# A decode block of attention and a gated MLP: no tile framework, the down projection's first 16 row chunks in two loads, its last two row chunks in pieces

## The chip, the core and the metric

The kernel runs on one core of a Trainium2 chip. A core has five engines with queues of their own: PE multiplies matrices (its weight loads are shown as PEld), DVE and ACT work on vectors, POOL on constants here, and SP issues the transfers. PE writes into PSUM, banks of 2 KB a partition; everything else lies in SBUF, 128 partitions wide. Transfers from memory run on 16 DMA engines beside the five, and engines tell each other of finished work by semaphores. The metric is the device time of one execution in microseconds (us). Beside it stands the span, from the first to the last instruction that the profile shows.

## The reference, cut to what matters

```python
def reference(A_x, A_k_cache, A_v_cache, A_wq, A_wo, B_x, B_w_gate, B_w_up, B_w_down):
    x = A_x                                    # 8 x 1 x 1024, float32
    h = x + A(layernorm(x))                    # 32 heads of 128, 4 of keys and values, last 1024 keys
    return h + B(layernorm(h))

def A(x):
    q = (x @ wq) by heads
    scores = einsum("bhqd,bhkd->bhqk", q, k) * 128 ** -0.5
    o = einsum("bhqk,bhkd->bhqd", softmax(scores), v)
    return o @ wo

def B(x):                                      # w_gate, w_up 1024 x 3584, w_down 3584 x 1024
    return (gelu(x @ w_gate) * (x @ w_up)) @ w_down
```

There are 8 rows in the batch, so each weight and each cached key and value is used for few products: the kernel reads some 111 MB and computes little on each byte.

## The kernel before, in words

**Stages.** Layer norm of x; the q projection (`wq`, two loads of 8 MiB); scores for two halves of the heads (`kt`, two loads of 8 MiB); softmax; the product with the values (`v`, two of 8 MiB); the output projection (`wo`, two of 8 MiB); the residual sum `h_sb` and its layer norm; gate and up projections for a first set of 4 x 512 columns and a second of 3 x 512 (`gu`, two loads of 8 MiB and two of 6 MiB), each followed by gelu on ACT, a product on DVE, transposes on PE and a copy into `at`; and the down projection. Every matmul has 32 columns of weights (8 batch rows, repeated four times) and writes a quarter of the PSUM partitions; four such matmuls, one for each quarter, run side by side. Each float32 matmul stands in the profile as two records.

**The down projection.** `w_down` has 28 chunks of 128 rows. `PARTS` says how many chunks a load holds: 16 in the first (`head`, 8 MiB, line 60 through `load`), then 4, 4, 2, 1 and 1 (`rest`, line 274). Chunks 0 to 23 are multiplied at line 283 in four quarters of 512 columns into `d1_ps`, two chunks at a time; DVE copies that to `d1` (line 288). The last four chunks (`TAIL`) are multiplied at line 297 with 256 columns in each quarter into `d_ps`, to which line 291 adds `h_sb` and line 303 adds `d1`. DVE copies `d_ps` to `o_fin` (line 308), and line 309 writes it out.

**What sets the order.** All loads are issued by SP in one queue, in the order of the code. The weights share two SBUF buffers (the pool `wts`), so a load is issued when PE has done its last matmul on the load before the last. While one buffer is worked on, the other is being filled. The tile framework works out the waits; the order on each engine is mostly that of the code, but its scheduler has put line 291 ahead of the second layer norm's transposes and the first transposes of the softmax between the two score groups. At the end it waits on all semaphores, brings all engines to a barrier, clears the semaphores on POOL and brings them to a barrier again (line 366).

## Time and profile before

| | us |
|---|---|
| median of 3 runs | 268.02 (267.89 to 268.24) |
| profiled execution | 268.06 |
| its span | 266.2 |
| PE busy | 138.2 |
| DVE busy | 25.1 |
| first 16 chunks of the down projection landed | 247.05 |
| PE's last matmuls end | 262.61 |

In the profile, "DMA share" is the mean share of 16 DMA engines that are at work. "PEclk" is the clock that PE was granted, as a share of the full one; a busy PE at half clock does half the work. In rows of the timeline the first number is the start, the second the length, and the bracket says how long the engine was idle before and what ended that. In the chain that ended last each piece is followed back to what released it. "xN" counts records. SPq is SP's queue, on which an issue takes about 0.35 us.

### The profile page before, as it was taken

Reading aid. Unit: us, or ns where it says so; the run is one execution under the profiler, and the core shown is the slowest. Engines: PE = TensorE matmul, PEld = TensorE weight load, DVE = VectorE, ACT = ScalarE, POOL = GpSimd, SP = SyncE. Lnnn points to the kernel's source line nnn. Section 1 sums busy time; section 2 is a strip of 40 time slices with the busy share of each in tenths; the row PEclk is TensorE's granted clock in tenths of the full one; section 3 lists DMA queues with packets and bytes.
Section 4 is the critical chain, followed back from the end, with each engine's and each line's share of the span. In section 5 each row is a group of like instructions: output and inputs, shape, how many; then the busy total and the mean of one; then the engine's idle time right before and its main releaser. Section 6 shows DMA issues by size and latency. Waiting matters only on the chain.

```text
span 266.2 us, 2036 instructions
## 1 busy us (share of the span) xinstructions
PE 138.2 (52%) x934; PEld 38.2 (14%) x934; DVE 25.1 (9%) x57; ACT 10.3 (4%) x14; POOL 2.7 (1%) x9
## 2 busy tenths in 40 slices
PE   0000986805836616607608609629319494760894
PEld 0000321201121111101102102112002120110221
DVE  2004010100120110200200000340000200010001
ACT  1002000000020120000000000020000000000000
POOL 4000000000000000000000000000000000000000
PEclk9999995985966965965955957986856868596599
DMA  8997999899989998999899989998999999998991
GB/s 315 473 473 320 473 473 416 374 473 463 433 364 473 455 453 354 465 453 453 364 463 453 446 374 453 453 453 377 443 401 458 450 394 475 433 414 384 426 402 70
DMA packets 2759, 111.43 MB, mean 419 GB/s; under 512 B 312, under 2 KB 440, under 8 KB 704
## 3 DMA queue, kind: packets, MB, share of 16 engines
q1 hardware_dynamic: 2752, 111.31, 97.2%
q8 instruction: 7, 0.11, 0.2%
HBM read 111.18 MB, written 0.13 MB: 418 GB/s over the span
## 4 chain that ended last, share of the span: by engine, by line
DMA 69%; PE 28%; DVE 2%; issue 0%; SPq 0%; ACT 0%
DMA gu<-gu 20%; DMA wo<-wo 11%; DMA v<-v 11%; DMA kt<-kt 9%; DMA wd<-dn 9%; DMA x_sb<-x 8%; PE gu_ps L249 7%; PE d_ps L283 5%; PE y_ps L226 4%; PE q_ps L132 4%; PE s_ps L157 4%; PE o_ps L202 3%; PE d_ps L297 1%; DVE ln_bn L102 0%; PE ln_pt L95 0%
## 5 line engine op out<-in xcount | busy, mean ns | idle before, releaser
L249 PE MATMUL gu_ps<-gu,ln_t 128*32 128x512 f32 x224 | 37.7, 757 | 19.8 <-DMA gu<-gu 19.8
L226 PE MATMUL y_ps<-wo,ot 128*32 128x512 f32 x128 | 18.7, 749 | 17.5 <-DMA wo<-wo 17.5
L202 PE MATMUL o_ps<-v,pt 128*32 128x512 f32 x128 | 18.2, 733 | 15.1 <-DMA v<-v 15.1
L157 PE MATMUL s_ps<-kt,qz 128*32 128x512 f32 x128 | 18.0, 725 | 13.6 <-DMA kt<-kt 13.6
L132 PE MATMUL q_ps<-wq,ln_t 128*32 128x512 f32 x128 | 19.3, 771 | 3.4 <-DMA wq<-wq 2.9
L283 PE MATMUL d_ps<-wd,at 128*32 128x512 f32 x96 | 13.0, 707 | 8.4 <-DMA wd<-dn 8.4
L95 PE MATMUL ln_pt<-ident,ln_xn 8*128 8x8 f32 x16 | 1.6, 224 | 29.8 <-DVE ln_xn L119 29.8
L249 PEld LDWEIGHTS gu_ps<-gu,ln_t 128*32 128x32 f32 x224 | 9.2, 135 | 46.8 <-issue 27.2
L226 PEld LDWEIGHTS y_ps<-wo,ot 128*32 128x32 f32 x128 | 4.8, 133 | 30.7 <-issue 22.6
L202 PEld LDWEIGHTS o_ps<-v,pt 128*32 128x32 f32 x128 | 4.5, 133 | 27.4 <-DMA v<-v 15.5
L157 PEld LDWEIGHTS s_ps<-kt,qz 128*32 128x32 f32 x128 | 4.7, 131 | 25.8 <-issue 16.2
L95 PE MATMUL pp<-ident,p 128*128 128x128 f32 x16 | 3.5, 361 | 6.7 <-ACT p L166 5.2
L132 PEld LDWEIGHTS q_ps<-wq,ln_t 128*32 128x32 f32 x128 | 4.6, 137 | 16.6 <-issue 12.9
L257 DVE TENSOR_TENSOR hm<-ge,gu_ps 128x512 f32<-128x512 f32 (+1 forms) x2 | 1.4, 686 | 57.7 <-ACT ge L255 57.7
L95 PEld LDWEIGHTS ln_pt<-ident,ln_xn 8*128 8x128 f32 x16 | 1.5, 175 | 30.2 <-issue 30.2
L283 PEld LDWEIGHTS d_ps<-wd,at 128*32 128x32 f32 x96 | 3.2, 126 | 17.4 <-issue 8.9
L163 DVE TENSOR_REDUCE nmax<-s_ps 128x1 f32<-128x1024 f32 x2 | 2.5, 1225 | 32.4 <-PE s_ps L157 32.4
L166 ACT ACTIVATE p<-s_ps,nmax 128x1024 f32<-128x1024 f32 x2 | 2.2, 1115 | 60.8 <-DVE nmax L163 60.8
L108 ACT ACTIVATE ln_sd<-ln_ve 8x1 f32<-8x1 f32 x2 | 0.4, 202 | 100.1 <-DVE ln_ve L106 100.1
L233 DVE COPY y_sb<-y_ps 128x512 f32<-128x512 f32 x1 | 0.7, 691 | 35.4 <-PE y_ps L226 35.4
L208 DVE TENSOR_SCALAR o<-o_ps,share 128x128 f32<-128x128 f32 x2 | 0.7, 352 | 33.3 <-PE o_ps L202 33.3
L95 PEld LDWEIGHTS pp<-ident,p 128*128 128x128 f32 x16 | 2.3, 179 | 9.2 <-ACT p L166 7.0
(53 smaller groups left out, 45.5 us busy)
## 6 DMA issues: line engine op xcount, KB each, us to landing
gu<-gu SPq DMA_DIRECT2D x2, 6144.0 KB, 21.7
wd<-dn SPq DMA_DIRECT2D x2, 2048.0 KB, 17.4
wd<-dn SPq DMA_DIRECT2D x1, 1024.0 KB, 21.7
wd<-dn SPq DMA_DIRECT2D x2, 512.0 KB, 23.2
out<-o_fin SPq DMA_DIRECT2D x1, 128.0 KB, 1.7
wq<-wq SPq DMA_DIRECT2D x2, 31.4
x_sb<-x SPq DMA_DIRECT2D x1, 32.0 KB
kt<-kt SPq DMA_DIRECT2D x2, 27.3
```

What stands on the lines that cost most here:

```text
L95: nc.tensor.transpose(pt[:, i, :], src[:, i * P:(i + 1) * P], ident[:rows, :rows])
L132: nc.tensor.matmul(q_ps[32 * j:32 * j + 32, :], xt[c], wq_t[hf][:, c, j * N:(j + 1) * N], start=(c == 0), stop=(c == NC - 1),)
L157: nc.tensor.matmul(s_ps[32 * r:32 * r + 32, k0:k0 + N], qz[hf][:, s, at:at + 32], k_t[:, s, half * HB + b, k0:k0 + N], start=(b == 0), sto ...
L163: nc.vector.tensor_reduce(out=nmax, in_=s_ps, axis=AX.X, op=ALU.max, negate=True)
L166: nc.scalar.activation(p_sb, s_ps, AF.Exp, bias=nmax, accum_out=tot)
L202: nc.tensor.matmul(o_ps[32 * r:32 * r + 32], pt[:, c, 32 * r:32 * r + 32], v_t[:, s, c, half * HB:(half + 1) * HB, :], start=(c == 0), sto ...
L208: nc.vector.tensor_scalar(o_sb, o_ps[:, 0], share[:, 0:1], None, op0=ALU.mult)
L226: nc.tensor.matmul(y_ps[32 * r:32 * r + 32, :], ot[:, 2 * hf * REP + h + e].rearrange("p r b -> p (r b)"), w[:, h + e, ch * N:(ch + 1) * N ...
L249: nc.tensor.matmul(pair[32 * j:32 * j + 32, s, :], ht[c], w[:, c, j * N:(j + 1) * N], start=(c == 0), stop=(c == NC - 1),)
L257: nc.vector.tensor_mul(hm[:rows], ge[:rows], pair[:rows, 1, :])
L283: nc.tensor.matmul(d1_ps[32 * r:32 * r + 32, :], at[:, q + e, :], rows_of(q + e)[:, ch * N:(ch + 1) * N], start=(q == 0), stop=(q == first ...
L297: nc.tensor.matmul(d_ps[32 * j:32 * j + 32, :], at[:, q, :], rows_of(q)[:, j * QW:(j + 1) * QW], start=False, stop=(q == last),)
```

## The change

The program is written on the engines' own queues. A small class, `Flow`, keeps one counting semaphore for each compute engine and one for each transfer; `run` appends an instruction with the waits that its engine has not yet made, and `move` a transfer. Loads, buffers and matmuls up to the gate and up projections are the same; the constants `spread` and `add2` are made on POOL, the transposes of p follow both score groups, and line 291's product with `h_sb` comes after chunk 23. There is no barrier at the end: SP waits for the outputs and clears the semaphores.

In the down projection, `PARTS` now holds 8, 8, 4, 4, 2 and 1 chunks: the first 16 are two loads into the same buffer. Chunk 26, the last but one, is loaded in three transfers over partitions 0 to 111, 112 to 119 and 120 to 127 (`SHARES`); its matmuls wait for all three. The last chunk is laid out by the host in three blocks of columns (`ENDS`): of each quarter's 256 columns the first 128, then 64, then 64, a transfer each, with 2 KB, 1 KB and 1 KB a row. The sum of the last four chunks stands in two PSUM banks, `acc` for the first 128 columns of each quarter and `tb` for the others, so every group of four matmuls of 256 columns is two groups of 128. ACT copies the first half and DVE the second, and each is written out by its own transfer.

```diff
--- before.py
+++ after.py
...
-PARTS = (16, 4, 4, 2, 1, 1)
+
+PARTS = (8, 8, 4, 4, 2, 1)
+HEAD = 16
+SHARES = (112, 120, P)
+ENDS = (128, 64, 64)
 TAIL = 4
...
-@with_exitstack
-def decode_block(ctx: ExitStack, tc: tile.TileContext, x, wq, kt, v, wo, gu, dn, out):
...
-    nc = tc.nc
+class Flow:
...
+    def missing(self, engine, waits):
+        need = {}
+        for w in waits:
+            if w is None:
+                continue
+            s, v = w
+            if self.seen.get((engine, s.name), 0) < v and need.get(s.name, (s, 0))[1] < v:
+                need[s.name] = (s, v)
+        for s, v in need.values():
+            self.seen[engine, s.name] = v
+        return list(need.values())
+
+    def start(self, engine, make, waits):
+        need = self.missing(engine, waits)
+        for s, v in need[:-1]:
+            getattr(self.nc, engine).wait_ge(s, v)
+        ins = make(getattr(self.nc, engine))
+        for s, v in need[-1:]:
+            ins.wait_op(s, v, "sem-ge")
+        return ins
+
+    def run(self, engine, make, *waits, mark=True):
+        ins = self.start(engine, make, waits)
+        if not mark:
+            return None
+        self.done[engine] += 1
+        ins.then_inc(self.own[engine], 1)
+        return self.own[engine], self.done[engine]
+
+    def move(self, name, out, src, *waits, engine="sync"):
+        s = self.sem(name)
+        self.start(engine, lambda e: e.dma_start(out, src), waits).then_inc(s, 16)
+        return s, 16
+
...
+def decode_block(nc, x, wq, kt, v, wo, gu, dn, ends, outs):
...
+    fl = Flow(nc)
+    run, move = fl.run, fl.move
...
-    def load(src, shape, name):
-        t = wts.tile(shape, F32, tag="w", name=name)
-        nc.sync.dma_start(t, src)
-        return t
...
+    BUF = NC * SET
+    wbuf = [sb(f"w{i}", P, BUF) for i in range(2)]
+    free = [None, None]
+    turn = [0]
+
+    def buffer():
+        i = turn[0] % 2
+        turn[0] += 1
+        return i, wbuf[i]
+
+    def load(src, name, letters, **sizes):
+
+        i, buf = buffer()
+        n = 1
+        for s in src.shape[1:]:
+            n *= s
+        t = buf[:, 0:n].rearrange(f"p ({letters}) -> p {letters}", **sizes)
+        return t, move(name, t, src, free[i]), i
...
+    spread = sb("spread", P, CP, B)
+    run("gpsimd", lambda e: e.tensor_copy(
+        spread, ident[:, 0:B].unsqueeze(1).to_broadcast([P, CP, B])), id_ok)
+
+    add2 = sb("add2", P, 2, 32)
+    consts = run("gpsimd", lambda e: e.tensor_add(
+        add2.rearrange("p c m -> p (c m)"), ident[:, 0:2 * 32], ident[:, 2 * 32:4 * 32]))
...
+        p0, tok0 = transposes(ta, p_sb[:, 0:W // 2], KC // 2, p_ok, ta_free)
+        ta_free = run("vector", lambda e: e.tensor_copy(pt[:, 0:KC // 2, :], p0), tok0)
+        p1, tok1 = transposes(ya, p_sb[:, W // 2:W], KC // 2, p_ok, ya_free)
+        ya_free = run("scalar", lambda e: e.copy(pt[:, KC // 2:KC, :], p1), tok1)
...
+            ta_free = heads_out(0, *o_first, ta_free)
+            heads.append(ta_free)
...
-    d1_ps = ps_y.tile([P, N], F32, tag="y", name="d1_ps")
-    d_ps = ps_a.tile([P, QW], F32, tag="a", name="d_ps")
-    head = load(dn[0], [P, PARTS[0], D], "wd0")
-    rest = wts.tile([P, DF // P - PARTS[0], D], F32, tag="w", name="wd1")
-    q0 = PARTS[0]
-    for n, src in zip(PARTS[1:], dn[1:]):
-        nc.sync.dma_start(rest[:, q0 - PARTS[0]:q0 - PARTS[0] + n], src)
+    bufs = []
+    for n in (HEAD, DF // P - HEAD):
+        i, buf = buffer()
+        bufs.append((free[i], buf[:, 0:n * D].rearrange("p (q n) -> p q n", n=D)))
+
+    def chunks(q, n=1):
+        clear, buf = bufs[q >= HEAD]
+        q -= HEAD * (q >= HEAD)
+        return clear, buf[:, q:q + n]
+
+    def rows_of(q):
+        return chunks(q)[1][:, 0]
+
+    arrived = {}
+    q0 = 0
+    for i, n in enumerate(PARTS):
+        clear, t = chunks(q0, n)
+        ends_at = SHARES if n == 1 else (P,)
+        here, p0 = [], 0
+        for p1 in ends_at:
+            here.append(move(f"wd{i}_{p0}", t[p0:p1], dn[i][p0:p1], clear))
+            p0 = p1
+        arrived.update((q, here) for q in range(q0, q0 + n))
         q0 += n
-
-    def rows_of(q):
-        return head[:, q] if q < PARTS[0] else rest[:, q - PARTS[0]]
+    blocks = []
+    c0 = 0
+    for i, (n, src) in enumerate(zip(ENDS, ends)):
+        t = rows_of(last)[:, NQ * c0:NQ * (c0 + n)]
+        blocks.append((c0, n, t, move(f"we{i}", t, src)))
+        c0 += n
 
     for q in range(0, first, 2):
         for r in range(NQ):
-            e, ch = divmod(r, 2)
-            nc.tensor.matmul(
-                d1_ps[32 * r:32 * r + 32, :], at[:, q + e, :], rows_of(q + e)[:, ch * N:(ch + 1) * N],
-                start=(q == 0), stop=(q == first - 2),
-            )
-    d1 = work.tile([P, N], F32, tag="two", name="d1")
-    nc.vector.tensor_copy(d1, d1_ps)
-
-    for j in range(NQ):
-        nc.tensor.matmul(
-            d_ps[32 * j:32 * j + 32, :], spread.rearrange("p r b -> p (r b)"),
-            h_sb[:, j * QW:(j + 1) * QW], start=True, stop=False,
-        )
-    for q in range(first, last + 1):
+            e2, ch = divmod(r, 2)
+            tok = run("tensor", lambda e: e.matmul(
+                ya[32 * r:32 * r + 32, :], at[:, q + e2, :],
+                rows_of(q + e2)[:, ch * N:(ch + 1) * N],
+                start=(q == 0), stop=(q == first - 2)),
+                *arrived[q + e2], at_ok[(q + e2) * P >= SETS[0] * N], ya_free,
+                mark=(q == first - 2 and r == NQ - 1))
+    d1 = sb("d1", P, N)
+    d1_ok = run("vector", lambda e: e.tensor_copy(d1, ya), tok)
+
+
+    cut = ENDS[0]
+    halves = [(acc[:, 0:cut], 0, cut), (tb[:, 0:QW - cut], cut, QW)]
+
+    def add(lhs, rhs, *waits, start=False):
+
+        for d_ps, a, b in halves:
+            for j in range(NQ):
+                run("tensor", lambda e: e.matmul(
+                    d_ps[32 * j:32 * j + 32, :], lhs(j), rhs(j)[:, a:b], start=start, stop=False),
+                    *waits, mark=False)
+
+    add(lambda j: spread.rearrange("p r b -> p (r b)"), lambda j: h_sb[:, j * QW:(j + 1) * QW],
+        h_ok, consts, start=True)
+    for q in range(first, last):
+        add(lambda j: at[:, q, :], lambda j: rows_of(q)[:, j * QW:(j + 1) * QW], *arrived[q], at_ok[1])
+        if q == first + 1:
+            add(lambda j: add2[:, j // 2, :], lambda j: d1[:, (j % 2) * QW:(j % 2) * QW + QW], d1_ok)
+    o_fin = sb("o_fin", P, QW)
+    done = []
+    for i, (c0, n, t, here) in enumerate(blocks):
+        d_ps, a, b = halves[i > 0]
         for j in range(NQ):
-            nc.tensor.matmul(
-                d_ps[32 * j:32 * j + 32, :], at[:, q, :], rows_of(q)[:, j * QW:(j + 1) * QW],
-                start=False, stop=(q == last),
-            )
-        if q == first + 1:
-            for j in range(NQ):
-                nc.tensor.matmul(
-                    d_ps[32 * j:32 * j + 32, :], add2[:, j // 2, :],
-                    d1[:, (j % 2) * QW:(j % 2) * QW + QW], start=False, stop=False,
-                )
-    o_fin = const.tile([P, QW], F32, name="o_fin")
-    nc.vector.tensor_copy(o_fin, d_ps)
-    nc.sync.dma_start(out, o_fin)
+            tok = run("tensor", lambda e: e.matmul(
+                d_ps[32 * j:32 * j + 32, c0 - a:c0 - a + n], at[:, last, :], t[:, j * n:(j + 1) * n],
+                start=False, stop=(c0 + n == b)), here, mark=(j == NQ - 1))
+        if c0 + n == b:
+            make = (lambda e: e.copy(o_fin[:, a:b], d_ps)) if i == 0 else (
+                lambda e: e.tensor_copy(o_fin[:, a:b], d_ps))
+            done.append(run(("scalar", "vector")[i > 0], make, tok))
+    sent = [move("out0", outs[0], o_fin[:, 0:cut], done[0]),
+            move("out1", outs[1], o_fin[:, cut:QW], done[1])]
+    for s, val in sent:
+        nc.sync.wait_ge(s, val)
+
+    ids = sorted(s.num for s in fl.sems)
+    assert ids == list(range(ids[0], ids[0] + len(ids)))
+    nc.sync.sem_clear(range(ids[0], ids[-1] + 1))
...
+    cuts = [sum(ENDS[:i]) for i in range(len(ENDS) + 1)]
+    by_group = rows[-1].reshape(P, NQ, QW)
+    ends = np.concatenate([by_group[:, :, a:b].reshape(-1) for a, b in zip(cuts, cuts[1:])])
...
-    out = nc.dram_tensor("out", (P, QW), F32, kind="ExternalOutput").ap()
+    out = nc.dram_tensor("out", (P * QW,), F32, kind="ExternalOutput").ap()
+    cut = P * ENDS[0]
+    outs = [o.rearrange("(p n) -> p n", p=P) for o in (out[0:cut], out[cut:P * QW])]
```

Two places of the program show what moved. On SP, from the last load of the up projection to the end, this stood before (`wd` is the SBUF buffer of the down projection, `dn` its weights in memory, sizes are partitions x elements):

```order
L60 DMA gu_1_631<-gu 128x12288 [waits DMAHW2_49,PE_49]
L60 DMA wd_669<-dn 128x16384 [waits DMAHW3_49,PE_49]
L274 DMA wd_671<-dn 128x4096 [waits DMAHW4_49,PE_49]
L274 DMA wd_671<-dn 128x4096
L274 DMA wd_671<-dn 128x2048
L274 DMA wd_671<-dn 128x1024 x2
L309 DMA out<-o_fin 128x256 [waits DVE_49]
L366 UNCONDITIONAL_BRANCH
```

And now, from the first load of the down projection (`w` is either buffer, `ends` the last chunk in its new layout):

```order
L85 DMA w<-dn 128x8192 [waits tensor_done]
L85 DMA w<-dn 128x8192
L85 DMA w<-dn 128x4096 [waits tensor_done]
L85 DMA w<-dn 128x4096
L85 DMA w<-dn 128x2048
L85 DMA w<-dn 112x1024
L85 DMA w<-dn 8x1024 x2
L85 DMA w<-ends 128x512
L85 DMA w<-ends 128x256 x2
L85 DMA out<-o_fin 128x128 [waits scalar_done]
L85 DMA out<-o_fin 128x128 [waits vector_done]
L448 ISA [waits out1_done,out0_done]
```

One load of 16 chunks has become two of 8, the last two loads have become six, the output is two transfers, and a clear of the semaphores (the ISA row) follows on SP.

On PE, from chunk 24 on, before (`d_ps` is the PSUM sum, `at` the gated activations):

```order
L297 MATMUL d_ps<-wd_671,at 32x256 [waits DMAHW0_49]
L297 MATMUL d_ps<-wd_671,at 32x256 x7
L303 MATMUL d_ps<-d_725,add_98 32x256 [waits DVE_49]
L303 MATMUL d_ps<-d_725,add_98 32x256 x3
L297 MATMUL d_ps<-wd_671,at 32x256 [waits DMAHW1_49]
L297 MATMUL d_ps<-wd_671,at 32x256 x3
L297 MATMUL d_ps<-wd_671,at 32x256 [waits DMAHW2_49]
```

And now, from the second half of the sum of `d1` on; the last row is followed by three more of its kind:

```order
L419 MATMUL tb<-d,add 32x128 x4
L419 MATMUL acc<-w,at 32x128 [waits wd5_112_done,wd5_0_done,wd5_120_done]
L419 MATMUL acc<-w,at 32x128 x3
L419 MATMUL tb<-w,at 32x128 x4
L434 MATMUL acc<-w,at 32x128 [waits we0_done]
L434 MATMUL acc<-w,at 32x128 x3
L434 MATMUL tb<-w,at 32x64 [waits we1_done]
L434 MATMUL tb<-w,at 32x64 x3
L434 MATMUL tb<-w,at 32x64 [waits we2_done]
```

Chunk 26 waits for its three shares, and the last chunk's single wait has become three, each ahead of four narrower matmuls.

More of the change, by code (lines that the diff above doesn't have):

```diff
@@ L179, in heads_out @@
+    ot = sb("ot", P, HQ, CP, B)
+    def heads_out(hf, o_sb, ready, clear):
+        t, tok = transposes(ta, o_sb, 1, ready, clear)
+        op = t.rearrange("p o m -> p (o m)")
         for s in range(2):
```

334 lines of the change are left out of this document (180 added, 154 removed).

## The prediction

> **What bounds the kernel now.** I read the page first, for the shares; then the stretches, for what the loads move in each; then the chain that ended last, for the end of the program; then the timeline and the rows of single lines, for prices.
>
> ```profile
> span 266.2 us, 2036 instructions
> q1 hardware_dynamic: 2752, 111.31, 97.2%
> DMA 69%; PE 28%; DVE 2%; issue 0%; SPq 0%; ACT 0%
> ```
>
> One queue carries 111.31 MB and its packets fill 97.2% of the time of the 16 DMA engines. The 28% that the chain gives to PE must be read with care: while PE works on one weight buffer the other is being filled, so the chain walks through PE though the loads never pause. The stretches show that:
>
> ```profile
> core 0: us, PE busy (x) PEld busy (x) DVE busy (x) ACT busy (x) POOL busy (x), PEclk, DMA share, GB/s
> 1.75:228.00 226.25, 113.44 (x749) 31.59 (x752) 22.74 (x53) 8.70 (x13) 1.54 (x3) 0.77 1.00 432
> 247.10:260.10 13.00, 13.00 (x100) 3.46 (x104) 0.00 (x0) 0.00 (x0) 0.00 (x0) 0.80 0.98 408
> 260.10:262.00 1.90, 1.90 (x40) 0.73 (x32) 0.69 (x1) 0.00 (x0) 0.00 (x0) 1.00 0.26 103
> 262.00:266.20 4.20, 0.57 (x10) 0.08 (x8) 0.42 (x1) 0.00 (x0) 0.00 (x0) 0.96 0.09 31
> ```
>
> From 1.75 to 228 us the DMA share is 1.00 at 432 GB/s. Nothing that only rearranges the engines in there can gain, as long as the next load is always waiting in the queue. At the end the share drops to 0.26 while some DMA engines still finish, and after 262 us nothing is loaded. So there are three places to win: the 1.75 us ahead of the stream, the ragged end near 261 us, and the 4.2 us behind the last load.
>
> ```profile
> 222.73 24.33 DMA wd<-dn
> ...
> 247.10 13.02 PE d_ps L283 x96
> 260.12 0.86 PE d_ps L297 x16
> 260.98 0.60 PE d_ps L303 x8
> 261.58 1.03 PE d_ps L297 x16
> ```
>
> ```profile
> 261.93 0.16 PEld L297 LDWEIGHTS d_ps<-wd,at 128*32 128x32 f32 x8 [0.40 <-DMA wd<-dn]
> 263.09 0.35 SPq L309 DMA_DIRECT2D out<-o_fin  x1
> out<-o_fin SPq DMA_DIRECT2D x1, 128.0 KB, 1.7
> L366 SPq EVENT_SEMAPHORE  x7: 17/28/28, 264.8 to 266.2; - x7
> L366 POOLq EVENT_SEMAPHORE_RANGE_CLEAR  x1: 96/96/96, 265.5 to 265.5; - x1
> ```
>
> The first 16 chunks of the down projection land in one load at 247.05, and PE then runs without a pause to 261.6, where it waits 0.40 us for the last chunk, which is there at 261.93. PE and the loads end almost together. The last matmuls end at 262.61, the copy takes 0.42 (its row is below), the output is issued at 263.09 and has landed at 264.8. From there to 266.2 there are only semaphores and a clear of them: 1.4 us.
>
> **The change, part by part.** The sum is made against the profiled execution, 268.06 us, of which 266.2 are the span and 1.86 lie around it; the median of the runs is 268.02, so the two agree within 0.04.
>
> *The stream.* The weight loads keep their order, sizes and two buffers; each waits for PE's last matmul on its buffer, as before. Whether a load is late is read from these:
>
> ```profile
> 222.73 0.33 SPq L60 DMA_DIRECT2D wd<-dn  x1
> 227.74 9.03 PE L249 MATMUL gu_ps<-gu,ln_t 128*32 128x512 f32 x48 [5.07 <-DMA gu<-gu]
> 236.82 2.27 SPq L274 DMA_DIRECT2D wd<-dn  x5
> 238.19 0.55 PE L95 MATMUL hp<-ident,hm 96*128 96x96 f32 x4 [1.43 <-DVE hm L257]
> ```
>
> The load issued at 222.73 has to follow one that lands at 227.74: 5.0 us of cover. The five issued from 236.82 follow one that lands at 247.05: 10.2 us. Nine issues instead of five cost 4 x 0.45 (2.27 / 5) = 1.8 us on SP's queue and use 1.8 of that cover. The new order of transposes and copies in the middle (both score groups ahead of the first transposes of p) delays PE by single microseconds under the same cover. I put all of it at nothing; if a load came late, each microsecond beyond 5 would cost one. The other engines' constants move from DVE to POOL in the first 5 us, where PE has nothing to do before 28 us: nothing.
>
> *The two loads of 8 chunks.* The first half lands after half of 16 x 512 KiB, which at 432 GB/s is 9.7 us ahead of 247.05, at 237.3. PE is busy with the transposes at 238.19 until 238.74; then it can do chunks 0 to 7, which cost 32 of the 96 records. PE's debt at 247.05 so falls by a third. That would let it follow the loads, but it also inserts waits, and PE's clock reacts to waits:
>
> ```profile
> 50.80:54.20 3.40, 1.79 (x16) 0.54 (x8) 1.05 (x3) 0.00 (x0) 0.00 (x0) 1.00 1.38 598
> 54.20:57.60 3.40, 0.00 (x0) 0.00 (x0) 0.00 (x0) 0.00 (x0) 0.00 (x0) 1.00 0.76 328
> 57.60:61.00 3.40, 0.00 (x0) 0.00 (x0) 0.00 (x0) 0.00 (x0) 0.00 (x0) 0.51 1.07 463
> 71.30:74.70 3.40, 1.06 (x12) 0.12 (x4) 1.23 (x1) 1.01 (x1) 0.00 (x0) 1.00 0.76 328
> 74.70:78.10 3.40, 2.23 (x8) 1.44 (x8) 1.08 (x3) 0.29 (x3) 0.00 (x0) 0.50 1.38 598
> 248.80:252.20 3.40, 3.40 (x20) 0.79 (x16) 0.00 (x0) 0.00 (x0) 0.00 (x0) 0.50 0.97 414
> 252.20:255.60 3.40, 3.40 (x36) 0.96 (x32) 0.00 (x0) 0.00 (x0) 0.00 (x0) 1.00 1.00 424
> ```
>
> ```profile
> 249.66 0.20 PEld L283 LDWEIGHTS d_ps<-wd,at 128*32 128x32 f32 x4 [0.66 <-issue]
> 250.51 0.20 PEld L283 LDWEIGHTS d_ps<-wd,at 128*32 128x32 f32 x4 [0.66 <-issue]
> ...
> 258.66 0.12 PEld L283 LDWEIGHTS d_ps<-wd,at 128*32 128x32 f32 x4 [0.31 <-issue]
> 259.09 0.12 PEld L283 LDWEIGHTS d_ps<-wd,at 128*32 128x32 f32 x4 [0.31 <-issue]
> ```
>
> The granted clock moves in steps of 3.4 us. A stretch with 1.79 us of work keeps 1.00; one with 1.06, or none, is followed by 0.50; a full one is followed by 1.00. Four records of 512 columns take 0.85 us at 0.50 (249.66 to 250.51) and 0.43 at 1.00 (258.66 to 259.09). At 408 to 432 GB/s, 2 MiB take 4.9 to 5.1 us, so the loads behind 247.05 land near 252.0 (chunks 16 to 19), 256.9 (20 to 23), 259.3 (24, 25), 260.6 (26) and 261.9 (27). PE starts chunks 8 to 15 at 247.05 at half clock, needs 5 to 6 us for them, takes 1.7 for 16 to 19, is done between 254 and 255, and waits 2 to 3 us for 256.9. Then stand 1.7 us for chunks 20 to 23 and six groups of 256 columns at 0.43 (260.12 to 260.98 is two): h, chunks 24 and 25, d1, 26, 27; 4.3 us at full clock. With the clock kept, PE is through by 261.2 and only waits for the last load. If the wait costs it the clock, a step of 3.4 us goes at half speed, and it ends 1.7 us later, at 262.9: PE and no longer the last load is the end. The place of the steps decides. With those of this profile (252.2, 255.6, 259.0), chunk 15 is done at 253.1, chunk 19 at 254.8, and both stretches hold over 2 us of work: kept. For other places: a wait of 2.9 us leaves both its stretches over about 1.6 us of work only where a step cuts it near its middle (a piece of 1.1 to 1.8 us, 0.7 of 3.4, 2 places of 10); where the first rise comes late, the wait is shorter, which adds about 2 of 10. So the clock is lost at 6 of 10. [...]
>
> *The last chunk in three blocks, PSUM in two halves.* At full clock the last block is 64 columns where it was 256: of 0.68 us (261.93 to 262.61) it saves up to three quarters of the 0.43 that columns take, 0.32. The copy on DVE and the cost of a narrower one:
>
> ```profile
> L308 DVE COPY o_fin<-d_ps 128x256 f32<-128x256 f32 x1 | 0.4, 425 | 1.7 <-PE d_ps L297 1.7
> L288 DVE COPY d<-d_ps 128x512 f32<-128x512 f32 x1 | 0.7, 692 | 20.9 <-PE d_ps L283 20.9
> L196 ACT COPY pt<-pp 128x512 f32<-128x512 f32 x2 | 1.2, 586 | 5.3 <-PE pp L95 5.3
> ```
>
> 692 - 425 = 267 ns for 256 columns, so 128 columns take 425 - 133 = 292 ns: a gain of 0.13. ACT copies the other half while PE ends; under 0.6 us, beside. Its output issue (0.35 on SP) goes ahead of the second one; if PE's two halves end within 0.2 us of each other, the second is held back by up to 0.15. The output that ends last is half as large: of 1.7 us I take off 0.05, bounds 0 and 0.15 (64 KB at 432 GB/s).
>
> *Shares of 112, 8 and 8, blocks of 2 KB and 1 KB a row.* More and smaller pieces on the stream's last 1.2 us. The trace has one load of 8 partitions, x, queued behind the first weight load:
>
> ```profile
> 1.17 21.88 DMA x_sb<-x
> L60 SPq EVENT_SEMAPHORE  x11: 17/17/28, 22.9 to 213.2; - x11
> ```
>
> The weight load ahead of it released SP at 22.9, x was there at 23.05: 0.15 us for 32 KB, which is one 4 KB row on a DMA engine at 432/16 GB/s. So eight rows go to eight engines, side by side. Two such shares give some engines one row more than an even split and others one less: 0.15 us later where the late engines get them, 0.15 earlier where the others do. The page does not say which engines are late; I take 0 and keep both. For the smaller rows I take 0.1, bounds 0 and 0.3.
>
> *The exit.* The chain of semaphores, drains, barriers and the clear from 264.8 to 266.2 goes; a wait for two outputs and one clear on SP (0.1 by the clear's row, plus 0.05) stay: a gain of 1.25, bounds 0.9 and 1.4.
>
> Sum, clock lost: PE's last matmul ends at 263.05 (262.9 and the 0.15 that a matmul takes to drain) for 262.61, +0.44; second output held, the middle of its bounds, +0.07; copy -0.13; output -0.05; exit -1.25. Together -0.92: 267.1. Clock kept: last load +0.1, matmuls -0.32, copy, output and exit as before: -1.65, 266.4.
>
> **The rivals.** *Clock kept*, 266.4: spoken for by the steps of this profile, against by their width of 4 in 10. *The exit is only moved*: if the device's time outside the span grows by what the span loses, 267.1 + 1.25 = 268.3, no change; the 1.86 us outside are not in the trace, so nothing excludes it. *Small loads pay a fixed price in series*, the one on the other side: the output's 128 KB take 1.7 us where 432 GB/s would need 0.3, so 1.4 each; four loads more on the last stretch would be +5.6, 272.7, slower. From 0.25 us per load it eats the gain. The x row (0.15 us behind its neighbour) speaks against it, since loads that are queued overlap that price; only the last of them pays it, and did before. [...]
>
> **How the numbers follow.** Clock lost 0.50, clock kept 0.36 (6 to 4 by the places, moved a little to the second because this profile's own steps keep it), exit only moved 0.06, small loads in series 0.04; 0.04 for a load that comes late in the middle, slower too. Under about 0.2% (0.54 us) a measurement of this kernel cannot be told from no change. The first two are faster by more than that, save for a part of the first (an exit gain of 0.9 and the late shares make 267.1 into 267.6): faster 0.83, same 0.09, slower 0.08. The range goes from the kept clock with its better ends (-0.15 shares, -0.15 exit) to the lost clock with its worse: 266.1 to 267.6.
>
> **What would show it.** In the profile after: DMA share still 1.00 at 432 GB/s to 228 us; PE working near 239 us and waiting before 252, before 256.9; the granted clock of the stretch from 256 to 260 (0.50 for the forecast) and no wait for the last load at the end (PE still behind), or 1.00 and a wait at each of the last loads; the last copy near 0.29 us; some 0.2 us from the output's landing to the end of the span. I am wrong if the time from the last landing to the end stays over a microsecond, if the last loads land later than 262.4, or if the stream shows a share under 0.95 anywhere before 240.

## The result, and the profile after

The changed kernel takes 268.34 us (median of 12 runs, 267.64 to 270.38), the kernel before 268.06 (12 runs, 267.89 to 268.39). The ratio is 1.0015, with a 95% interval of 1.0002 to 1.0028. By the prediction's measure of 0.2% that is no change, where 267.1 was forecast. The profiled execution took 268.78 us, 267.2 of them the span.

The page's lines on the span, the load queue and the chain that ended last, and then the stretches of the changed kernel (columns as before: start and end, length, the engines' busy time, PEclk, DMA share, GB/s):

```profile
span 267.2 us, 2120 instructions
q1 hardware_dynamic: 3344, 111.31, 97.9%
DMA 76%; PE 21%; SPq 1%; issue 0%; DVE 0%
```

```profile
1.75:228.00 226.25, 110.42 (x741) 31.94 (x744) 20.99 (x50) 9.18 (x14) 2.02 (x5) 0.80 1.00 431
254.00:256.00 2.00, 0.66 (x8) 0.00 (x0) 0.00 (x0) 0.00 (x0) 0.00 (x0) 1.00 1.01 422
256.00:258.00 2.00, 1.24 (x12) 0.42 (x16) 0.00 (x0) 0.00 (x0) 0.00 (x0) 1.00 0.98 371
258.00:260.00 2.00, 1.12 (x24) 0.48 (x16) 0.69 (x1) 0.00 (x0) 0.00 (x0) 1.00 1.03 183
260.00:262.00 2.00, 0.92 (x35) 0.92 (x38) 0.00 (x0) 0.00 (x0) 0.00 (x0) 0.99 1.01 194
262.00:264.00 2.00, 1.94 (x43) 1.42 (x34) 0.00 (x0) 0.00 (x0) 0.00 (x0) 0.50 0.41 124
```

The same stretches of the kernel before:

```profile
258.00:260.00 2.00, 2.00 (x24) 0.53 (x20) 0.00 (x0) 0.00 (x0) 0.00 (x0) 1.00 0.94 379
260.00:262.00 2.00, 2.00 (x40) 0.80 (x36) 0.69 (x1) 0.00 (x0) 0.00 (x0) 1.00 0.27 109
```

Up to 256 us the stream is what it was (431 GB/s to 228 us, 432 before). Then, for four microseconds, the DMA engines are as busy as ever (share 1.01 to 1.03) and move half as much: 183 and 194 GB/s. A share of 1 with half the bytes is the line to learn: the engines are at work all the time, and the transfers advance at half their rate. The timeline of the changed kernel shows who waits for it, and its groups the exit:

```profile
237.77 3.64 PE L402 MATMUL ya<-w,at 128*32 128x512 f32 x32
256.76 1.92 PE L402 MATMUL ya<-w,at 128*32 128x512 f32 x16 [2.10 <-DMA w<-dn]
261.08 0.42 PE L419 MATMUL acc<-w,at 128*32 128x128 f32 x8 [1.96 <-DMA w<-dn]
263.13 0.20 PEld L419 LDWEIGHTS acc<-w,at 128*32 128x32 f32 x8 [0.51 <-DMA w<-dn]
264.41 0.65 PE L434 MATMUL tb<-w,at 128*32 128x64 f32 x16
265.00 0.82 SPq L85 DMA_DIRECT2D out<-o_fin  x2
265.13 0.29 DVE L439 COPY o_fin<-tb 128x128 f32<-128x128 f32 x1 [5.69 <-PE tb L434]
```

```profile
out<-o_fin SPq DMA_DIRECT2D x2, 64.0 KB, 1.6
L448 SPq EVENT_SEMAPHORE_RANGE_CLEAR  x1: 78/78/78, 267.1 to 267.1; - x1
```

Chunks 24 and 25 let PE go on at 261.08 and chunk 26 at 263.13, where the prediction had 259.3 and 260.6. Chunks 24 and 25 are loaded over all partitions and stand ahead of the shares in the queue; they are late too. From the second output's landing (issued at 265.45, landed after 1.6 us) to the end are 0.15 us. The exit's gain came; the last loads took it back.

### The profile page after: what moved, and what is told of

Same layout as the page of the kernel before. It is cut to its first block, busy times and chain, and to the rows that moved or that the text cites. A ratio compares the mean times of both kernels' runs of the same rounds, so it can differ in the third digit from the quotient of the medians.

```text
span 267.2 us, 2120 instructions
## 1 busy us (share of the span) xinstructions
PE 136.9 (51%) x990; PEld 41.0 (15%) x990; DVE 23.5 (9%) x55; ACT 10.5 (4%) x15; POOL 3.2 (1%) x11
## 4 chain that ended last, share of the span: by engine, by line
DMA 76%; PE 21%; SPq 1%; issue 0%; DVE 0%
DMA w<-gu 18%; DMA w<-wq 15%; DMA w<-kt 12%; DMA w<-wo 11%; DMA w<-v 11%; DMA w<-dn 9%; PE big L346 7%; PE big L241 4%; PE tb L288 3%; PE tb L213 3%; PE ya L316 3%; SPq L85 1%; PE acc L419 0%; PE tb L434 0%; PE acc L434 0%
## 5 line engine op out<-in xcount | busy, mean ns | idle before, releaser
L346 PE MATMUL big<-w,ln_t 128*32 128x512 f32 x224 | 37.1, 747 | 20.8 <-DMA w<-gu 20.8
L241 PE MATMUL big<-w,qz 128*32 128x512 f32 x128 | 19.0, 761 | 20.6 <-DMA w<-kt 20.6
L316 PE MATMUL ya<-w,ot 128*32 128x512 f32 x128 | 18.4, 738 | 19.3 <-DMA w<-wo 19.3
L402 PE MATMUL ya<-w,at 128*32 128x512 f32 x96 | 13.3, 702 | 7.7 <-DMA w<-dn 7.7
L346 PEld LDWEIGHTS big<-w,ln_t 128*32 128x32 f32 x224 | 9.1, 133 | 47.4 <-issue 26.8
L288 PE MATMUL tb<-w,pt 128*32 128x512 f32 x64 | 9.2, 741 | 9.7 <-DMA w<-v 9.7
L288 PE MATMUL acc<-w,pt 128*32 128x512 f32 x64 | 8.7, 700 | 8.5 <-DMA w<-v 8.5
L213 PE MATMUL tb<-w,ln_t 128*32 128x512 f32 x64 | 8.8, 711 | 3.0 <-DMA w<-wq 3.0
L316 PEld LDWEIGHTS ya<-w,ot 128*32 128x32 f32 x128 | 5.1, 133 | 31.1 <-issue 31.1
L213 PE MATMUL acc<-w,ln_t 128*32 128x512 f32 x64 | 9.5, 762 | 0.5 <-DVE ln_t L199 0.5
```

What stands on the lines that cost most here:

```text
L213: tok = run("tensor", lambda e, c=c, j=j: e.matmul(q_ps[32 * j:32 * j + 32, :], xt[c], w[:, c, j * N:(j + 1) * N], start=(c == 0), stop=(c ...
L241: tok = run("tensor", lambda e: e.matmul(s_ps[32 * r:32 * r + 32, k0:k0 + N], qz[hf][:, s, c0:c0 + 32], k_t[:, s, half * HB + b, k0:k0 + N ...
L288: tok = run("tensor", lambda e: e.matmul(o3[32 * r:32 * r + 32], pt[:, c, 32 * r:32 * r + 32], v_t[:, s, c, half * HB:(half + 1) * HB, :], ...
L316: tok = run("tensor", lambda e: e.matmul(ya[32 * r:32 * r + 32, :], ot[:, 2 * hf * REP + h + e2].rearrange("p r b -> p (r b)"), w[:, h + e ...
L346: tok = run("tensor", lambda e: e.matmul(pair[32 * j:32 * j + 32, s, :], ht[c], w[:, c, j * N:(j + 1) * N], start=(c == 0), stop=(c == NC ...
L402: tok = run("tensor", lambda e: e.matmul(ya[32 * r:32 * r + 32, :], at[:, q + e2, :], rows_of(q + e2)[:, ch * N:(ch + 1) * N], start=(q == ...
```

## Experiments: what slows the last loads

Three suspects lie on that stretch: the shares, the three small blocks of the last chunk, and the mere number of small transfers.

**e1_even**, the shares undone:

```diff
-SHARES = (112, 120, P)
+SHARES = (P,)
```

> The changed kernel with chunk 26 in one load over all 128 partitions again; all else as changed. Theory A (transfers over 112 and 8 partitions give the DMA engines partitions of their neighbours, and they slow each other to half rate): over 380 GB/s up to 259 us, the last load landed near 262.0 instead of past 263.9, time 266.2 to 267.3, about 0.995 of before, faster. Theory B (the small rows of the last chunk's blocks are slow): the rate still falls below 220 GB/s in 258 to 262, time 268.0 to 268.6. Theory C (too many small transfers one behind the other, whatever their shape): two transfers fewer, about a third of the loss back, 267.5 to 268.

Measured: 266.76 us (265.69 to 268.43, 12 runs), ratio 0.9956 (0.9936 to 0.9975). Its stretches:

```profile
258.00:260.00 2.00, 1.61 (x36) 0.74 (x32) 0.69 (x1) 0.00 (x0) 0.00 (x0) 1.00 0.93 357
260.00:262.00 2.00, 2.00 (x74) 1.64 (x66) 0.00 (x0) 0.00 (x0) 0.00 (x0) 1.00 0.32 118
```

Without the shares the rate stays up, and in the medians 1.6 us come back (268.34 to 266.76).

**e4_before_shares**, the shares alone, in the kernel before:

```diff
-        nc.sync.dma_start(rest[:, q0 - PARTS[0]:q0 - PARTS[0] + n], src)
+        shares = (0, 112, 120, P) if q0 == DF // P - 2 else (0, P)
+        for p0, p1 in zip(shares, shares[1:]):
+            nc.sync.dma_start(rest[p0:p1, q0 - PARTS[0]:q0 - PARTS[0] + n], src[p0:p1])
```

> The kernel before with only chunk 26 loaded in shares of 112, 8 and 8. A: the rate falls to about half from 258 on, the last load lands some 2 us later, time 269.5 to 270.5, 1.005 to 1.009 of before. B: 268.0 to 268.3, unchanged. C: two transfers more, 268.3 to 268.8.

Measured: 270.04 (269.77 to 270.48), ratio 1.0074 (1.0059 to 1.0088): 2.0 us slower, with the same stretch at half the rate:

```profile
256.00:258.00 2.00, 2.00 (x24) 0.60 (x20) 0.00 (x0) 0.00 (x0) 0.00 (x0) 1.00 1.04 346
258.00:260.00 2.00, 1.22 (x12) 0.12 (x4) 0.69 (x1) 0.00 (x0) 0.00 (x0) 1.00 1.01 201
260.00:262.00 2.00, 0.60 (x12) 0.42 (x16) 0.00 (x0) 0.00 (x0) 0.00 (x0) 1.00 0.85 195
```

**e2_one_end** keeps the shares and loads the last chunk in one transfer; **e3_columns** keeps the three transfers for chunk 26 but cuts it by columns, each over all partitions:

```diff
-        blocks.append((c0, n, t, move(f"we{i}", t, src)))
+    whole = move("we", rows_of(last), ends)
+        blocks.append((c0, n, t, whole))
```

```diff
-        for p1 in ends_at:
-            here.append(move(f"wd{i}_{p0}", t[p0:p1], dn[i][p0:p1], clear))
+        cols = (0, 512, 768, D) if n == 1 else (0, D)
+        for x0, x1 in zip(cols, cols[1:]):
+            here.append(move(f"wd{i}_{x0}", t[:, :, x0:x1], dn[i][:, :, x0:x1], clear))
```

> The changed kernel with the last chunk in one load of 4 KB rows (the host lays the three blocks side by side); chunk 26 still in shares of 112, 8 and 8. A: the rate still halves in 258 to 262, last load landed past 263.5, time 268.0 to 268.8, as the changed kernel. B: last load near 262, time 266.2 to 267.3. C: about a third of the loss back, 267.5 to 268.

> The changed kernel with chunk 26 still in three transfers, but each over all 128 partitions and a part of the columns (512, 256 and 256: rows of 2, 1 and 1 KB). A: no loss from it but some 0.1 us for the smaller rows: last load near 262.1, time 266.3 to 267.4. B and C: as the changed kernel or worse, 268.0 to 268.8.

Measured: e2 269.28 (268.90 to 269.46), ratio 1.0043 (1.003 to 1.0056), still 197 GB/s in both stretches (it lies 0.9 above the changed kernel, more than was expected; its profile has a late output, which comes up again below); e3 267.35 (265.73 to 269.00), ratio 0.9963 (0.9941 to 0.9986), and its rate stays up:

```profile
258.00:260.00 2.00, 2.00 (x12) 0.43 (x8) 0.00 (x0) 0.00 (x0) 0.00 (x0) 0.50 1.01 356
260.00:262.00 2.00, 2.00 (x72) 1.98 (x68) 0.69 (x1) 0.00 (x0) 0.00 (x0) 0.92 0.31 111
```

So neither the small rows nor the count of transfers slows the loads; the cut by partitions does. The first row also shows PE at half clock (0.50), lost in a wait that e1 passed with the clock kept (1.00 in its rows above).

**e5_halves** and **e6_112_16** ask what in the cut: an uneven one, shares of 8 partitions, or any cut.

```diff
-SHARES = (112, 120, P)
+SHARES = (64, P)        # e5_halves
+SHARES = (112, P)       # e6_112_16
```

> [...] A1 (what counts is that an engine gets other partitions than in the other loads): the rate falls to about 200 GB/s from 258 on as with 112, 8 and 8, time 267.8 to 269. A2 (what counts is the uneven number of rows and the loads that use 8 engines only): over 350 GB/s up to 259, last load near 262, time 266.2 to 267.4.

> [...] A1: slow as the changed kernel, 268 to 269. A2: fast, 266.2 to 267.4.

Measured: e5 269.68 (269.05 to 271.59), ratio 1.0073 (1.0044 to 1.0102), 200 and 213 GB/s from 260 to 264 us, though its two halves are even (above the 267.8 to 269 that were expected; the profile is of its longest run, in which PE's clock was 0.65 at most on this stretch); e6 268.33 (267.55 to 269.29), ratio 1.001 (0.9999 to 1.0021), 216 and 210 GB/s from 258 to 262, without a share of 8. Each of the three cuts by partitions does it.

**e11_middle_112** and **e12_middle_64** take it away from the end: in the kernel before, the last load of the up projection, 6 MiB in the middle of the stream, is cut (112 in the first, 64 in the second). The letters in these two expectations are explained there and are theories of their own.

```diff
-            w = load(gu[k][s], [P, NC, nb * N], f"gu{k}_{s}")
+            w = wts.tile([P, NC, nb * N], F32, tag="w", name=f"gu{k}_{s}")
+            shares = (0, 112, P) if (k, s) == (1, 1) else (0, P)
+            for p0, p1 in zip(shares, shares[1:]):
+                nc.sync.dma_start(w[p0:p1], gu[k][s][p0:p1])
```

> The kernel before, with the last load of the up projection (6 MiB, in the middle of the stream, near 208 to 222 us) in two: partitions 0 to 111 (5.25 MiB) and 112 to 127 (0.75 MiB). Theory A, loads over another number of partitions are slow by themselves: 5.25 MiB at the 200 to 220 GB/s of the end instead of 432 cost 12 us and the small one 1.8: 280 to 283, and a stretch of over 20 us at half the rate. Theory B, only two kinds of split in flight beside each other are slow: two changes of kind at up to 2.0 us each (the loss when chunk 26 alone was shared), 268.5 to 272, with the long load at over 400 GB/s in its middle. Theory C, it is a matter of the stream's last loads alone: 268.0.

> The same load in two halves of 64 partitions (3 MiB each). Theory A: 6 MiB at half the rate, 281 to 284. Theory B: two to three changes of kind, 268.5 to 274. Theory C: 268.0. [...]

Measured: 286.94 (286.10 to 287.77), ratio 1.069 (1.065 to 1.073), and 285.82 (285.77 to 285.87), ratio 1.065 (1.063 to 1.067). The pages' rows of GB/s, in 40 slices of about 7 us, first of e11 and then of e12:

```profile
GB/s 303 431 440 445 440 440 433 440 440 440 440 440 433 440 440 424 440 422 403 403 422 442 440 440 440 433 422 463 413 358 220 222 220 133 284 431 383 401 407 77
```

```profile
GB/s 295 443 443 448 443 443 436 443 443 443 434 434 362 415 434 445 443 434 434 434 443 436 443 443 443 427 434 399 436 339 222 224 215 226 323 434 372 418 400 68
```

A load over 64 or 112 partitions moves 215 to 226 GB/s in these slices, in mid-stream too, and the slice that holds the end of e11's, with its 16 partitions, moves 133. The loss is even dearer than expected (18.8 and 17.7 us, where 12 to 16 were): 6 MiB at 222 GB/s instead of 432 make 13.8 us, and where e12's other 4 us go was not followed.

A load over 64 partitions (e12, 215 to 226 GB/s) is about as slow as one over 112 (e11, 220 to 222), and no run here shows which DMA engine writes where. So the runs show what cut is slow, and why it is slow stays open.

## Experiments: the exit, the two loads, and the run-to-run spread

**e9_flow_only** keeps of the change only the program without framework; loads, PSUM sum, copy and output are as before, the product with `h_sb` early:

```diff
-PARTS = (8, 8, 4, 4, 2, 1)
-SHARES = (112, 120, P)
-ENDS = (128, 64, 64)
+PARTS = (16, 4, 4, 2, 1)
+SHARES = (P,)
+ENDS = (256,)
...
-    halves = [(acc[:, 0:cut], 0, cut), (tb[:, 0:QW - cut], cut, QW)]
+    halves = [(acc[:, 0:cut], 0, cut)]
...
-    sent = [move("out0", outs[0], o_fin[:, 0:cut], done[0]),
-            move("out1", outs[1], o_fin[:, cut:QW], done[1])]
+    sent = [move("out0", outs[0], o_fin, done[0])]
```

> The program on the engines' own queues and without barriers at the end, but with all loads, PSUM sum, copy and output as in the kernel before (16, 4, 4, 2, 1, 1 chunks, each over all partitions). The exit term of the prediction (1.25 us, bounds 0.9 to 1.4) alone: 266.8 us (266.6 to 267.1), span near 265, some 0.2 us from the output's landing to the end of the span, PE's last matmul within 0.3 us of 262.6. Rival 'the exit is only moved': 268.0, with the time outside the span near 3.1 us instead of 1.86. On the spread of 2 to 3 us that the kernels without the framework showed: if it comes from the changed tail (two loads of 8, three blocks, two outputs), the runs here lie within 0.8 us of each other; if it comes with the program without framework, over 1.2 us.

Measured: 266.28 (266.21 to 266.57), ratio 0.9925 (0.991 to 0.994). The tail of its timeline, and its clear:

```profile
262.64 0.42 DVE L438 COPY o_fin<-acc 128x256 f32<-128x256 f32 x1 [1.85 <-PE acc L434]
263.09 0.35 SPq L85 DMA_DIRECT2D out<-o_fin  x1
```

```profile
L445 SPq EVENT_SEMAPHORE_RANGE_CLEAR  x1: 72/72/72, 265.2 to 265.2; - x1
```

The output is issued at 263.09, as before, and landed after 2.0 us (1.7 before); the rest of the exit is gone. Beside the same chip's runs of before (268.15) the gain is 1.87 us: the spans are 1.45 shorter (266.4 to 264.95, medians) and the time outside them 0.5 (1.8 to 1.3). The exit did not move out of the span; a part outside went with it.

**e10_before_two_heads** (in the kernel before) and **e16_two_heads** (in e9) load the first 16 chunks in two loads of 8, and change nothing else (the diff is e16's, whose last chunk comes through `ENDS`; in e10 it is one more 1 at the end of `PARTS`); **e8_one_head** undoes it in e1:

```diff
-PARTS = (16, 4, 4, 2, 1)
+PARTS = (8, 8, 4, 4, 2, 1)
```

> The kernel before with only its first 16 chunks in two loads of 8. If two loads give PE pauses in which it loses its clock (the prediction's 'clock lost'), PE's last matmul ends up to 0.7 us later than before in some runs and the last block's copy with it: 268.1 to 268.9, with a spread over 1 us. If the split of the first 16 chunks matters to nothing behind it: 268.0 within 0.3, spread below 0.6. In both the loads still move over 400 GB/s from 247 to 259 us and the last load lands within 0.4 of 261.9.

> The same version with only the first 16 chunks in two loads of 8. In the kernel before, this alone left the median (268.18 against 268.15) and widened the runs to 1.9 us. If PE's pauses and the place of its clock steps make the spread: median 266.2 to 266.6 and a spread over 1.0 here too, the long runs by PE ending up to 1.7 us behind the last load. If not: 266.3 and under 0.6.

> The changed kernel with chunk 26 in one even load and the first 16 chunks in one load as before. PE then works without a pause from 247.05 to the end and its clock stays. Clock theory: PE ends near 262.8 in every run, 266.3 to 266.8 with a spread under 0.8 us, so the two loads of 8 chunks gain nothing in the median. Rival (the two loads are what gains, by PE's smaller debt): slower than the even variant by 0.5 or more, 267.3 and up.

Measured: e10 268.18 (267.82 to 269.75; before 268.15); e16 266.55 (266.35 to 266.58, where e9 had 266.28); e8 266.79 (265.55 to 267.49, where e1 had 266.76). By these medians two loads gain nothing and cost 0.0 to 0.3; the longest of e10's ten runs is 269.75.

**e7_warm** fills PE's pause in e1 with twelve matmuls whose result nothing uses:

```diff
+        if q == HEAD + 4:
+            for i in range(3):
+                for r in range(NQ):
+                    run("tensor", lambda e: e.matmul(
+                        big[0][32 * r:32 * r + 32, 0:N], at[:, 0, :], rows_of(0)[:, 0:N],
+                        start=True, stop=True), at_ok[1], mark=False)
```

> The changed kernel with chunk 26 in one even load, and three groups of four matmuls more on PE (into a PSUM bank that is free by then; they add nothing to the result) between chunk 19 and chunk 20, 2.6 us at full clock, where PE waits for a load. Clock theory (the runs of the even variant lie from 265.7 to 268.4 because PE's clock is lost in that wait in some runs): the upper group of runs goes, median 265.7 to 266.4, below the even variant's 266.76, the runs within 1.2 us. Rival (the spread comes from elsewhere, instruction loads near the end or the outputs): median 266.5 to 267.2 with the same spread of over 2 us.

Measured: 267.08 (266.46 to 267.74), ratio 0.9965 (0.9953 to 0.9978). The clock stayed at 1.00 from 256 to 264 us in its profile, to the end of PE's work, and the median is no better than e1's 266.76. So a clock kept in that pause does not by itself bring e1's shortest runs, 265.7. It does not clear the clock either: in this profile chunk 20 came late (PE went on at 258.46, e1 at 257.04).

What does? The versions with this tail and no shares (e1, e3, e7, e8) spread over 1.3 to 3.3 us, e9's four runs over 0.36. Four more runs take the parts of the tail one by one: **e13_early_base** is e8 with the product with `h_sb` moved to where e9 has it; **e14_two_outputs** is e13 with `ENDS = (128, 128)`; **e15_three_blocks** is e9 with `ENDS = (128, 64, 64)` into the one PSUM sum; **e16** is above.

> One load of 16, three blocks, two PSUM halves and two outputs, no shares, with the product with h_sb ahead of the gate projection, as in the kernel before, instead of behind chunk 23. It takes 0.43 us of full-clock matmuls off PE's last stretch. If PE ends last in the long runs of the version with the late product (265.6 to 267.5 there), the long group goes: 265.5 to 265.9, spread under 0.6. If the outputs or the blocks make the two groups, it stays: median near 266.8, spread over 1.2.

> The version without framework and with the old tail (266.28, 0.36 between its longest and shortest run), with only the last chunk's columns, the PSUM sum, the copy and the output in two halves of 128 (ACT and DVE copy, two outputs). By the prediction's terms: 0.21 less for the narrower last block, 0.13 for the copy, 0.05 for the output, 0.07 more for the held output: 266.0, spread under 0.6. If two outputs make the two groups of run times: spread over 1.2 and a median of 266.5 or more.

> The same version with only the last chunk's load and matmuls in three blocks of 128, 64 and 64 columns; one PSUM sum, one copy, one output. By the prediction's terms 0.1 more for the smaller rows, 0.32 less for the last block: 266.1, spread under 0.6. If the small loads at the end make the two groups: spread over 1.2.

Measured: e13 267.03 (265.69 to 268.11); e14 266.34 (265.57 to 266.96); e15 266.27 (266.09 to 266.45). Of these, the versions with two outputs spread (2.4 us over ten runs, 1.4 over five), and those with one do not (e15 0.4, e16 0.2, four runs each, too few to exclude a rare long one).

The profile of e13 is one of the long executions (267.45), that of e14 a short one (265.57). First e13, then e14, the output's issues in ns (shortest, median, longest) and the time from issue to landing:

```profile
L85 SPq DMA_DIRECT2D out<-o_fin x2: 348/816/1284, 263.1 to 263.5; - x2
DMA to landing us min/median/max: 2.4/2.4/2.5
```

```profile
L85 SPq DMA_DIRECT2D out<-o_fin x2: 344/346/348, 261.9 to 262.5; - x2
DMA to landing us min/median/max: 1.5/1.5/1.6
```

The pages' rows of the instruction loads (count, MB, share), e13 and then e14:

```profile
q8 instruction: 8, 0.13, 0.2%
```

```profile
q8 instruction: 7, 0.11, 0.2%
```

In the long one the second issue takes 1.28 us instead of 0.35, and the outputs land 2.4 to 2.5 us after their issues began instead of 1.5 to 1.6, with one instruction load of 16 KB more (0.11 MB for 7, 0.13 for 8). The profiles of e2 and e7 have an eighth load too. Their issues, e2 and then e7:

```profile
L85 SPq DMA_DIRECT2D out<-o_fin x2: 372/905/1438, 264.9 to 265.4; - x2
```

```profile
L85 SPq DMA_DIRECT2D out<-o_fin x2: 348/381/414, 263.5 to 264.1; - x2
```

The records of the three traces say when that load ran: from 263.01 to 264.38 in e13, 265.14 to 266.44 in e2, 263.17 to 264.11 in e7. In each the first issue takes its 0.35 to 0.37, and the second, which begins while the load runs, ends 0.36 to 0.38 after the load has ended. In e7 that costs 0.06 only, as the load was nearly over.

This is about half of what the long execution loses. The spans differ by 1.9 us (266.1 and 264.2), and e13's second issue begins 0.95 later than e14's. Of that, 0.8 is there before any output is issued: PE ends later, and DVE's last copy starts at 263.02 (e14: 262.21). The stretch that differs is this one, e13 and then e14:

```profile
250.20:253.60 3.40, 3.40 (x24) 0.75 (x20) 0.00 (x0) 0.00 (x0) 0.00 (x0) 0.59 0.98 419
```

```profile
250.20:253.60 3.40, 3.40 (x40) 0.95 (x32) 0.00 (x0) 0.00 (x0) 0.00 (x0) 1.00 1.01 429
```

Both have one load of 16 chunks and work through it without a pause, e13 at a granted clock of 0.59 and e14 at 1.00. e13's PE gets through 24 records where e14's gets through 40, meets no later load that it has to wait for, and is itself the end. The stretch ahead of it, from 246.8 us on, had 0.50 in e13 and 0.56 in e14, so by these means the clock rises to 1.00 about 3.2 us later in e13. The time of that rise is part of the spread, with the load kept in one.

**e17_two_queues** issues e14's first output on ACT's queue; **e18_one_output** keeps e14's halves and copies and sends one output behind both:

```diff
-    sent = [move("out0", outs[0], o_fin[:, 0:cut], done[0]),
+    sent = [move("out0", outs[0], o_fin[:, 0:cut], done[0], engine="scalar"),   # e17
...
+    sent = [move("out0", outs[0], o_fin, *done)]                                # e18
```

> The version with two halves and two outputs (265.57 to 266.96), with the first output issued on ACT's queue right behind ACT's copy, so that SP issues one output only. Where the second output was late, the profile shows its issue on SP at 1.28 us (with the late product) instead of 0.35 and one 16 KB instruction load more. If that load comes because SP's program runs on past the first output, SP now stands with one output as in the versions with one, which had 0.4 us of spread: 265.8, spread under 0.7, 7 instruction loads. If it is the count of small transfers at the end that delays an output, or PE's clock alone, nothing changes: 266.3, spread over 1.2.

> The same version with both halves of the last chunk, the PSUM sum and the copies, but one output behind both copies. If the second output makes the spread: under 0.6, and 266.1 to 266.3 (0.13 less than one copy of 256). If the two PSUM halves do (twice as many matmuls on PE's last stretch): spread over 1.2.

Measured: e17 265.65 (five runs from 265.52 to 265.74, one 267.10), ratio 0.991 (0.9889 to 0.993), where e14 has 0.9934 (0.9911 to 0.9958); e18 266.06 (five from 265.89 to 266.18, then 266.55 and 267.89), ratio 0.9915 (0.9899 to 0.993). In e17 both issues take their normal time:

```profile
L85 ACTq DMA_DIRECT2D out<-o_fin x1: 369/369/369, 262.4 to 262.4; - x1
L85 SPq DMA_DIRECT2D out<-o_fin x1: 348/348/348, 262.7 to 262.7; - x1
```

That SP is held by an instruction load when it issues a second output fits the three profiles with an eighth load; whose instructions it brings, and why it comes in some executions only, is not shown. The intervals of e14 and e17 overlap, so what speaks for the second queue is the count of long runs, one of six against three of five, and it is a small count. e18's profiled run (267.89), with one output, is long for another cause: its last load is late, against the same row of e14.

```profile
263.70 0.16 PEld L434 LDWEIGHTS tb<-w,at 128*32 128x32 f32 x8 [0.48 <-DMA w<-ends]
```

```profile
261.71 0.16 PEld L434 LDWEIGHTS tb<-w,at 128*32 128x32 f32 x8 [0.47 <-DMA w<-ends]
```

Two microseconds, on full loads over all partitions. The traces record sixteen steps for the landing of each transfer: in e18, from the load of chunks 20 to 23 on, fifteen are in time and the last comes 2.0 us behind them (258.68 against 256.67); in e7's late loads it is 1.4. What delays it stays open, and e17's long run was not profiled. e17 has the shortest median of all: 2.4 us less than the kernel before, without shares, with one load of 16 chunks, two halves and two queues for the outputs.

## Why the prediction was wrong

- **Shares of 112, 8 and 8: "I take 0 and keep both" (0.15 up or down). This step failed.** They cost 1.6 us in the change (268.34 against e1's 266.76) and 2.0 alone (e4). The working took them as eight rows on eight engines "side by side", from one load of 32 KB, x. Those 32 KB are too few to show a rate, and no run shows which engines a load's rows go to. A stream at 432 GB/s was assumed to be so whatever partitions a load covers; nothing in the trace of before had a large load over other than 128, and the bounds were too narrow for an unknown of that kind. The runs showed half the rate in its place, 183 and 194 GB/s for four microseconds, on chunk 26 and on the whole loads beside it: the half rate on chunk 26 alone (0.5 MiB) makes 1.2 us. The prediction's own mark for being wrong, a last load later than 262.4, is what came (PE waits for chunk 26 until 263.13).
- **The exit, 1.25 (0.9 to 1.4): right in kind, too small.** e9 measured 1.87, since 0.5 of the time outside the span went too. The span alone gave 1.45, just over the upper bound. The rival "only moved" is refuted.
- **The two loads of 8:** timing as foretold (first chunks at 237.77, a wait of 2.10 before 256.76 for "2 to 3 before 256.9"). The forecast was the lost clock, at 6 of 10; the profile after kept its clock through that wait, to 262 us, and lost it only behind the stretch from 258.57 to 261.98, which holds a wait of 1.96 us for the starved loads. The 6 of 10 rests on two estimates of the author: that a stretch with over about 1.6 us of work keeps the clock, and that each place of the steps is as likely as another. In the profile after, a stretch with 1.81 us of work kept it (255.15 to 258.57) and the one from 258.57, with 1.45, was followed by 0.50; where between them the bound lies, and how likely each place is, no run shows. Of the profiles with two loads, two lost it in that wait (e3, at 0.50 from 258 to 260, and e16) and five kept it (after, e1, e2 and e6 at 1.00 there, and e10; e5, with its lower clock, left out): too few for a share, but no support for 6 of 10. The price held where it was lost: in e3 PE's last matmul ends at 262.98, where the prediction had 263.05. In the medians the two loads cost 0.0 (e10) and 0.3 (e16).
- **The last block's 0.32:** not seen by itself; e15, with three blocks alone, gives 266.27 against 266.28. e18, with two blocks, two halves in PSUM, two copies and one output, lies 0.22 below e9.
- **The copy, 292 ns:** 0.29 measured. **The smaller rows, 0.1:** e15 shows none (266.27 against 266.28); e3, with more of them, lies 0.6 above e1, but its runs spread over 3.3 us and its profile has the lost clock. **Small loads in series**, 1.4 each, is refuted by e3, which has four loads more on the last stretch than the kernel before and is faster than it, and by e15, where two more cost nothing.
- **The second output, "held back by up to 0.15":** in the profile after nothing holds it (the copy ends at 265.42, the issue begins at 265.45). The sum took the issue itself as unchanged; that holds where SP is free (0.35), but under the instruction load it takes 1.28. In e13's profile that is about half of the 1.9 us to e14's, and PE's later end, by its clock, most of the rest. How they share what e1 (266.76) loses to e17 (265.65) is not shown, since no long run of e1 was profiled.

Without the shares the sum, 267.1, would have stood against 266.76. That it came near is partly luck, two errors of opposite sign: an exit that gave 0.6 more, and losses in the long runs (e1's 266.76 against e17's 265.65) for which the sum had no term.

## What to carry to other kernels

Cut a load by columns or by chunks, not by partitions: here loads over 112 or 64 partitions ran at half the rate, in the stream's end (183 to 216 GB/s) and in its middle (215 to 226, against 432), and whole loads beside them were late too. A DMA share of 1 is no proof of a full stream (here 1.03 at 183 GB/s); read the GB/s beside it. Drop closing barriers that nothing needs (e9, without framework and barriers, gained 1.87 us). Where two results leave at the end, try issuing them from two queues (five of six runs were short here, too few to be sure). And before a spread of 2 us is given one cause, look at a short and a long execution side by side: here three causes took part.

## What the runs showed of the hardware that was not expected

- Loads over 64 and 112 partitions ran at about the same rate in mid-stream, 215 to 226 GB/s (e12) and 220 to 222 (e11), against some 440 for 128 in the same pages.
- Where an instruction load of 16 KB was under way as SP began its second output issue, that issue ended 0.36 to 0.38 us after the load: 1.28 us instead of 0.35 in e13, 1.44 in e2, 0.41 in e7.
- Without the framework and its closing barriers the time outside the span fell as well, from 1.8 to 1.3 us (e9).
